# A wider second product of av, four warm-up products, combine weights kept once and the output in three column parts, under a new list of the first five engines

## The chip, the cores and the metric

The kernel runs on one core of one Trainium2 chip. The metric is the time of one execution on the device in microseconds (us), the median of several. TensorE is called PE below, its weight loads PEld, VectorE DVE, ScalarE ACT, GpSimd POOL, and SyncE, which issues all the DMAs of this kernel, SP.

## What is computed

Three stages follow one another on 3072 tokens of 512 columns, all in fp32.

```python
# attention: 4 batches x 8 heads x 768 tokens x 64; every query sees the keys within 16 of it
# and 24 block summaries (max of 32 keys, mean of 32 values)
a = softmax([mask(scale * q @ k.T), scale * q @ kmax.T + log(32)])
x = a @ [v, vmean]                          # then heads side by side: 3072 x 512
# dense layer, 512 -> 2048 -> 512
h = x @ w_in;  x = (h * cos(h)) @ w_out
# soft mixture of 8 experts with 4 slots each
logits = x @ phi                            # 3072 x 32
slots = softmax(logits, over tokens).T @ x  # 32 x 512
for e in range(8): out_e = relu(slots_e @ w1[e]) @ w2[e]      # 512 -> 1024 -> 512
y = softmax(logits, over slots) @ out       # 3072 x 512
```

## The kernel before

**Blocks and slots.** The tokens are cut into 6 blocks of 512, the 2048 hidden columns into 16 parts, which gives 96 slots s. A slot makes `h{s}a` and `h{s}c` (the product with `w_in`, lines 580, 581 and 588), `p`, `q` and `r` on DVE (lines 600, 604, 618), the sine `n{s}` and the cast `gh{s}` on ACT (608, 622), `gl{s}` on POOL (631) and `m{s}a`, `m{s}b` (the product with `w_out`). Each fp32 factor is split into a high part that ACT casts (`ih`, `oh`, line 553) and a low part (`il`, `ol`, line 560). Two PSUM banks hold the h products, so that `h{s+2}a` waits for `r{s}`.

**The sixteen weight parts** arrive as 1 MB loads `W{f}` and are unpacked during the first block by `ca`, `cb` on ACT (lines 134, 139), `cc` on DVE (148) and `cd` on POOL (156).

**Attention** runs in 24 groups. The first four (g = 0 to 3) have scores `sc{g}_{j}` (lines 327, 330), masking and maximum on DVE (`ev`, `mx`, lines 336, 344), exponentials in pieces of two query blocks on ACT (`ex`, line 366), a sum and reciprocal on DVE (`nm`), a normalisation on POOL (`nt`, line 456), transposes on PE (`tr`, 469) and their eviction (`aT`, 479). Then `av` multiplies by the 96 rows of values and `aw` by the 24 rows of block means, both at line 520: eight matmuls each per (g, j), with 64 columns. `xh` (ACT, line 536) and `xl` (DVE, 540) evict the result; `h0a` needs `xh` and `xl` of groups 0 and 2, `h0b` those of 1 and 3.

**The list.** Up to slot 80 the order of work of PE, DVE, ACT, POOL and SP is written out by hand: `ORDER` is a string of piece names, in which every engine executes its own pieces in the order in which they stand. The warm-up `fill_` (line 902) issues products of a matrix of ones; its four pieces f1, f11, f21 and f31 of ten matmuls stand ahead of `sc0_0` (two of them), behind `sc0_1` and behind `tr0_0`.

**The expert weights.** 64 blocks of 512 KB (`ex`) are loaded by `grab` into whatever space is free: 12 tiles that follow the attention's space when it closes, the spaces of xh and xl, those of the sixteen weight parts as the last block leaves them, 7 tiles of the ring, and x2 and x2T. The first 32 blocks are w1, the others w2. When a product has used a block, `release` either keeps its space for a later `place` or loads another block into it.

**The tail.** After the last slot come the logits and the softmax over tokens (the chain up to `slT`), `cT_mm` (transposes of the combine weights `call`, which stand there four times 32 columns wide: high, low, high, low), `hp_mm` (product with w1, line 1173), `relu`, `turn_h`, then the product with w2 in two halves of 256 columns (`yp_mm`, line 1219), `so_mm` (1239) and `combine` (line 1254, evicted at 1255, stored at 1256 as 512 KB with runs of 1024 bytes). Blocks 32 to 47 serve the first half and 48 to 63 the second.

Of the kernel before, what the change touches and what calls it, by code (L numbers as in the profile page):

```python
# [10 lines left out]
F32 = mybir.dt.float32  # L11
# [12 lines left out]
QB = 64  # L24
# [11 lines left out]
NFILL = 40  # L36
F0 = 10
# [8 lines left out]
NEXP = 12  # L46
# [27 lines left out]
def body(ctx: ExitStack, tc: tile.TileContext, q0, qk, kT, vT, vn, vx, w, phi, ex, cst, out):  # L74
# [430 lines left out]

    def first_av(g, j):
        first_x(g, j, grp[g]["v"][:KL, j], slice(0, KL))

    def first_aw(g, j):
        p = 2 * (g % 2) + j  # L510
        first_x(g, j, vsums[0][KL:KC, p:p + 1, :].to_broadcast([NSUM, 4, 128]), slice(KL, KC))

    def first_x(g, j, v, k):
        d = grp[g]
        if "av" not in d:
            d["av"], d["parts"] = bank(f"av{g}"), 0
        for u in range(4):
            for hh in range(2):
                r = slice(64 * hh, 64 * hh + 64)
                nc.tensor.matmul(d["av"][r, 256 * j + QB * u:256 * j + QB * u + QB], v[:, u, r],  # L520
                                 d["aT", j][k, 128 * u + 64 * hh:128 * u + 64 * hh + QB],
                                 start=d["parts"] == 0 and u == 0, stop=d["parts"] == 3 and u == 3)
        d["parts"] += 1

    def att_x(g):
        b, o = g // 4, 256 * ((g // 2) % 2)
        if b not in xh:
            xh[b] = xres.tile([128, 4, TB], F32R, name=f"xh{b}", tag="xh", bufs=2)
# [162 lines left out]
    call = m2.tile([128, 4 * NB, 4, 32], F32R, name="call", tag="call")  # L691
    run = {}

    def x2_out(j, t):
        do(f"xo{j}_{t}", x2_out_, t)

    def x2_out_(t):
        if x2 is None:
            m2_alloc_()
        if t % 2:  # L700
            return nc.scalar.mul(x2[:, t, :], acc[t], TWO_PI / W_SCALE)
        else:
            nc.vector.tensor_scalar_mul(x2[:, t, :], acc[t], TWO_PI / W_SCALE)
# [649 lines left out]
```

## Time and profile before

| | |
|---|---|
| median of 3 runs | 727.8 us (727.47 to 728.17) |
| the profiled execution | 730.21 us |
| its span, first to last instruction | 728.4 us |
| PE busy | 711.3 us (98%), 5260 matmul records |
| PEld busy | 560.0 us (77%) |
| DVE, ACT, POOL busy | 435.8 us, 411.5 us, 406.9 us |
| moved | 101.65 MB, of which HBM read 92.54 MB and written 6.29 MB |

The profiled execution took 1.8 us more than its span and 2.4 us more than the median of the runs. A busy share is an average over stages with different limits. An fp32 matmul leaves two records on PE, an fp32r matmul and a transpose one; matmuls are pipelined, so that the time per record is read from a run of them and not from the duration of one.

### The profile page before, as it was taken

The page shows a single profiled execution, that of the slowest core. Times are in us where ns is not written, and L with a number is a line of the kernel's source. Part 1 is how long each engine was busy: PE and PEld are TensorE (multiplying, and loading weights), DVE is VectorE, ACT ScalarE, POOL GpSimd, SP SyncE. Part 2 cuts the span into 40 slices and gives each one's busy share as a digit, 9 for nine tenths or more (in the row PEclk, how much of TensorE's full clock was granted, in tenths as well). Part 3 has the DMA queues.
Part 4 walks back from the last instruction along what each step waited for, and adds up shares of the span by engine and source line. Part 5 has one row for each costly group of instructions (what it writes and reads, how often), then busy time and mean ns, then how long its engine had stood idle before and what let it go on. Part 6 is the DMA issues. An engine that isn't in the chain of part 4 may idle for free.

```text
span 728.4 us, 13277 instructions
## 1 busy us (share of the span) xinstructions
PE 711.3 (98%) x5260; PEld 560.0 (77%) x5260; DVE 435.8 (60%) x680; ACT 411.5 (56%) x772; POOL 406.9 (56%) x310
## 2 busy tenths in 40 slices
PE   9899999999999999999999999999999999999994
PEld 9878777788887887787888787888787887787453
DVE  5678986974676574776574754674953444334323
ACT  4789997565554654654654754564735445434113
POOL 0756857766465565565673666674577665762000
PEclk9899999999999999999999999999999999999998
DMA  9976856402212301401302201301302822227998
GB/s 345 398 281 249 301 212 230 166 22 76 92 67 77 112 1 54 140 24 43 111 1 74 80 0 35 116 1 43 117 1 87 318 87 87 94 95 269 410 370 295
DMA packets 34862, 101.65 MB, mean 140 GB/s; under 512 B 3440, under 2 KB 13936, under 8 KB 32752
## 3 DMA queue, kind: packets, MB, share of 16 engines
q1 hardware_dynamic: 34800, 100.81, 38.1%
q8 instruction: 41, 0.67, 0.4%
q14 instruction: 21, 0.17, 0.1%
HBM read 92.54 MB, written 6.29 MB: 136 GB/s over the span
## 4 chain that ended last, share of the span: by engine, by line
PE 92%; ACT 4%; DVE 2%; issue 1%; POOL 0%
PE h L580 12%; PE h L581 12%; PE h L588 12%; PE acc L666 10%; PE acc L675 10%; PE acc L667 10%; PE tr L469 3%; PE av L504 3%; PE sc L384 2%; PE acc L652 2%; PE acc L653 2%; PE acc L655 2%; PE yp L1219 2%; PE hp L1173 2%; PE warmth L902 2%; PE av L520 1%
## 5 line engine op out<-in xcount | busy, mean ns | idle before, releaser
L631 POOL TENSOR_TENSOR gl<-a,gh 128x512 fp32r<-128x512 f32 x96 | 129.1, 1345 | 120.4 <-ACT gh L622 62.8
L560 POOL TENSOR_TENSOR wol<-w,woh 128x512 fp32r<-128x512 f32 x96 | 126.4, 1318 | 65.4 <-ACT woh L553 64.1
L580 PE MATMUL h<-xh,wih 128*128 128x512 f32 x384 | 155.4, 405 | 2.8 <-DVE a L618 2.8
L581 PE MATMUL h<-xl,wih 128*128 128x512 f32 x384 | 152.7, 398 | 0.0
L600 DVE TENSOR_SCALAR a<-h 128x512 f32<-128x512 f32 x96 | 66.0, 688 | 128.8 <-PE h L588 76.9
L608 ACT ACTIVATE a<-a,halfpi 128x512 f32<-128x512 f32 x96 | 69.4, 724 | 110.1 <-DVE a L604 109.8
L666 PE MATMUL acc<-woh,gh 128*128 128x512 f32 x320 | 127.4, 398 | 0.0
L667 PE MATMUL acc<-wol,gh 128*128 128x512 f32 x320 | 125.4, 392 | 0.0
L560 POOL TENSOR_TENSOR wil<-w,wih 128x512 fp32r<-128x512 f32 x81 | 106.9, 1323 | 30.0 <-PE h L588 11.4
L588 PE MATMUL h<-xh,wil 128*128 128x512 f32 x384 | 106.8, 401 | 0.0
L618 DVE TENSOR_TENSOR a<-h,a 128x512 f32<-128x512 f32 x96 | 65.9, 688 | 50.1 <-ACT a L608 50.1
L580 PEld LDWEIGHTS h<-xh,wih 128*128 128x128 f32 x384 | 72.3, 188 | 23.1 <-issue 3.7
L675 PE MATMUL acc<-woh,gl 128*128 128x512 f32 x320 | 88.3, 397 | 0.0
L581 PEld LDWEIGHTS h<-xl,wih 128*128 128x128 f32 x384 | 72.5, 189 | 16.0 <-DVE xl L540 0.5
L588 PEld LDWEIGHTS h<-xh,wil 128*128 128x128 f32 x384 | 71.0, 189 | 16.7 <-issue 1.0
L553 ACT CAST woh<-w 128x512 fp32r<-128x512 f32 x96 | 59.4, 619 | 32.1 <-PE acc L675 25.1
L553 ACT CAST wih<-w 128x512 fp32r<-128x512 f32 x96 | 59.3, 618 | 25.2 <-PE h L581 23.1
L622 ACT CAST gh<-a 128x512 fp32r<-128x512 f32 x96 | 58.9, 617 | 24.5 <-PE acc L667 19.1
L666 PEld LDWEIGHTS acc<-woh,gh 128*128 128x128 f32 x320 | 60.1, 188 | 14.4 <-issue 1.3
L667 PEld LDWEIGHTS acc<-wol,gh 128*128 128x128 f32 x320 | 60.2, 188 | 12.9
L675 PEld LDWEIGHTS acc<-woh,gl 128*128 128x128 f32 x320 | 58.8, 188 | 13.1 <-issue 0.6
L604 DVE SCALAR_TENSOR_TENSOR a<-a,h 128x512 f32<-128x512 f32 x96 | 65.5, 682 | 2.2
(156 smaller groups left out, 962.3 us busy)
## 6 DMA issues: line engine op xcount, KB each, us to landing
ex<-in_ex_dram SPq DMA_DIRECT2D x64, 512.0 KB
raw<-in_w_dram SPq DMA_DIRECT2D x16, 1024.0 KB
qk<-in_qk_dram SPq DMA_DIRECT2D x20, 736.0 KB
v<-in_vx_dram SPq DMA_DIRECT2D x24, 512.0 KB
kr<-in_kT_dram SPq DMA_DIRECT2D x16, 384.0 KB
out_dram<-o SPq DMA_DIRECT2D x12, 512.0 KB
vr<-in_vT_dram SPq DMA_DIRECT2D x12, 384.0 KB
v<-vs SPq DMA_DIRECT2D x40, 48.0 KB
```

The lines of the kernel that those rows point to most:

```text
L553: nc.scalar.copy(hi, W[f][:, part, :])
L560: (eng or nc.gpsimd).tensor_tensor(out=lo, in0=W[f][:, part, :], in1=hi, op=ALU.subtract)
L580: nc.tensor.matmul(h, hi[:, c], xh[s // NF][:, t, :], start=t == 0, stop=False)
L581: nc.tensor.matmul(h, hi[:, c], xl[s // NF][:, t, :], start=False, stop=False)
L588: nc.tensor.matmul(h, lo[:, c], xh[s // NF][:, t, :], start=False, stop=t == 3)
L600: nc.vector.tensor_scalar(out=a, in0=h, scalar1=0.25, scalar2=MAGIC, op0=ALU.add, op1=ALU.add)
L608: turn_dve["sin"] = nc.scalar.activation(a, a, AF.Sin, bias=halfpi, scale=-TWO_PI)
L618: nc.vector.tensor_tensor(out=a, in0=h, in1=a, op=ALU.mult)
L631: nc.gpsimd.tensor_tensor(out=gl, in0=a, in1=gh, op=ALU.subtract)
L666: nc.tensor.matmul(acc[t], gh[:, c], hi, start=f == 0, stop=False)
L667: nc.tensor.matmul(acc[t], gh[:, c], lo, start=False, stop=False)
L675: nc.tensor.matmul(acc[t], gl[:, c], hi, start=False, stop=f == NF - 1)
```

## The change

In the code, without the list:

```diff
-NFILL = 40
-F0 = 10
...
-NEXP = 12
+NEXP = 14
 NRING = 7
+PARTS = ((0, 256, 32), (256, 128, 48), (384, 128, 56))
...
     def first_av(g, j):
-        first_x(g, j, grp[g]["v"][:KL, j], slice(0, KL))
...
+                nc.tensor.matmul(d["av"][r, 256 * j + QB * u:256 * j + QB * u + QB], d["v"][:KL, j, u, r],
+                                 d["aT", j][:KL, 128 * u + 64 * hh:128 * u + 64 * hh + QB],
+                                 start=d["parts"] == 1 and u == 0, stop=False)
+
+    def first_aw(g, j):
+        d = grp[g]
         d["parts"] += 1
+        for hh in range(2):
+            r = slice(64 * hh, 64 * hh + 64)
+            a = d["aT", j][KL:KC, :].rearrange("p (u h c) -> p u h c", u=4, h=2)[:, :, hh, :]
+            nc.tensor.matmul(d["av"][r, 256 * j:256 * j + 256].rearrange("p (u c) -> p u c", u=4),
+                             vsums[0][KL:KC, 2 * (g % 2) + j, r], a, start=False, stop=d["parts"] == 4)
...
-    call = m2.tile([128, 4 * NB, 4, 32], F32R, name="call", tag="call")
+    call = m2.tile([128, 4 * NB, 2, 32], F32R, name="call", tag="call")
...
     def fill(n):
-        for i in range(0, n, 10):
-            do(f"f{i + (n > F0)}", fill_, min(10, n - i))
+        for i, k in enumerate((3,1,)):
+            do(f"f{i}", fill_, k)
 
     def fill_(n):
-        for i in range(n):
-            nc.tensor.matmul(warmth[:, 0:128], ones, ones, start=True, stop=True)
+        for _ in range(n):
+            nc.tensor.matmul(warmth, ones, ones.unsqueeze(1).to_broadcast([128, 4, 128]), start=True, stop=True)
...
         for i in range(NEXP):
             grab(exp_pool, f"e{i}")
+        grab(m2, "cT1")
...
-    for i in range(NRING):
+    for i in range(NRING + 1):
         grab(tail, f"r{i}")
...
     def cT_out(j):
-        o = cT[j // 2][:, 512 * (j % 2):512 * (j % 2) + 512]
-        (nc.scalar.copy if j % 2 else nc.vector.tensor_copy)(o, cps.pop(j))
+        o, ps = cT[j // 2][:, 512 * (j % 2):512 * (j % 2) + 512], cps.pop(j)
+        nc.vector.tensor_copy(o[0:64], ps[0:64])
+        nc.scalar.copy(o[64:128], ps[0:64])
...
-    cT_out(0)
-    cT_out(1)
     chain.__exit__(None, None, None)
...
-            release(16 * g + 4 * k + j, 2)
+            release(16 * g + 4 * k + j, 2 if g or k else 3)
...
     hp_mm(0, 0)
-    cT.append(place("cT2", F32R))
-    for j in range(2, 5):
+    cT += [place(f"cT{i}", F32R) for i in range(3)]
+    for j in range(5):
         cT_out(j)
...
-            u = 32 + 16 * h + 8 * g + 4 * (k // 4)
+            u = u0 + 4 * (8 // nk) * g + 4 * (k // nk)
...
-                                 eu[u + j][0][:, 256 * (k % 4):256 * (k % 4) + 256], start=k == 0, stop=k == 7)
-            if k % 4 == 3:
+                                 eu[u + j][0][:, w * (k % nk):w * (k % nk) + w], start=k == 0, stop=k == 7)
+            if k % nk == nk - 1:
...
     y_out(0, 1)
-    yp_mm(1, 0, range(2))
+    yp_mm(1, 0, range(4))
     so_mm(0, 0)
     so_mm(0, 1)
-    yp_mm(1, 0, range(2, 6))
+    yp_mm(1, 0, range(4, 8))
+    y_out(1, 0)
+    yp_mm(1, 1, range(3))
     for i in range(3):
         combine(0, i)
...
+    yp_mm(1, 1, range(3, 8))
     y_out(1, 1)
+    combine(0, 3)
     so_mm(1, 0)
     so_mm(1, 1)
-    for i in range(6):
-        combine(1, i)
+    combine(0, 4)
+    combine(0, 5)
+    yp_mm(2, 0, range(4))
+    combine(1, 0)
+    yp_mm(2, 0, range(4, 8))
+    y_out(2, 0)
+    yp_mm(2, 1, range(8))
+    y_out(2, 1)
+    combine(1, 1)
+    so_mm(2, 0)
+    so_mm(2, 1)
+    combine(1, 2)
+    for i in range(3):
+        combine(2, i)
```

So the second product `aw` issues two matmuls of 256 columns per (g, j) where it issued eight of 64. The warm-up is four matmuls of 512 columns, all ahead of `sc0_0`, where it was forty of 128 in four places. The combine weights stand once as high and low (64 columns), `cT_out` copies each turned block twice, and all three cT tiles take the places of blocks that the first `hp_mm` has used; this leaves room for two more `e` tiles, one more tile of the ring and one expert block at cT1's place. The output columns go as 256, 128 and 128: a `combine` of the last two parts makes eight products of 128 columns and stores 512 KB in runs of 512 bytes.

The new list holds the same pieces but for the warm-ups. The heads of three engines' lists, before (-) and after (+):

```diff
-PE  f1 f11 sc0_0 sc2_0 sc0_1 f21 sc2_1 sc1_0 sc1_1 sc3_1 sc3_0 tr0_0 f31 tr2_1 tr0_1 tr2_0 vs0_0 ...
+PE  f0 f1 sc0_0 sc0_1 sc2_0 sc2_1 sc1_0 sc1_1 tr0_0 sc3_0 sc3_1 vs0_0 tr0_1 vs0_1 vs0_2 av0_0 tr2_0 ...
-ACT ... ex3_0_0 aT0_1 cb1 xh2 xh0 ih0 aT1_1 ca2 aT3_1 cb2 ih1 xh3 xh1 ca3 cb3 ca4 cb4 ih2 y4_1 y4_0 n0
+ACT ... ex3_0_1 aT0_1 ca1 ih0 oh0 xh0 cb1 aT3_1 aT1_1 xh2 ca2 cb2 ih1 xh3 y4_1 xh1 y4_0 ca3 cb3 ih2 ca4 cb4 n0
-SP  K0 Q0 Q2 K1 C0 Q1 K3 C720 C848 K2 W0 K4 Q3 b0_0 W1 b0_2 b0_1 V2 V0 K5 V1 W2 V3 W3 W4 K6 G4 N G5 W5
+SP  K0 Q0 K1 C0 C848 Q2 K2 Q1 C720 K3 W0 V0 Q3 b0_0 b0_1 b0_2 V1 V2 W1 V3 K4 W2 G4 W3 W4 K5 G5 N W5
```

Up to `n8` ACT's list holds the same 112 pieces as before, in another order; up to `h10a` PE's list holds the same 85 pieces beside the warm-ups. On DVE, around `n8`, the list was `nm7 u9 q9 r8` and is `q9 r8 nm7 il10 nt7 r9 u9`.

## Rows read from the trace of the kernel before

**Rows 1.** Busy time by stage: stretch, engines (x instructions), granted PE clock, DMA share, GB/s.
```profile
0.00:41.20 41.20, 38.21 (x673) 36.47 (x674) 23.94 (x46) 24.94 (x81) 16.02 (x18) 0.92 0.92 353
41.20:104.00 62.80, 60.94 (x433) 47.42 (x433) 55.77 (x82) 62.34 (x138) 43.94 (x26) 1.00 0.74 268
104.00:110.00 6.00, 4.92 (x26) 3.72 (x28) 4.85 (x8) 4.88 (x7) 2.72 (x3) 0.72 0.51 194
...
250.00:400.00 150.00, 150.00 (x984) 119.68 (x983) 93.87 (x142) 83.50 (x140) 86.62 (x68) 1.00 0.17 57
680.00:700.00 20.00, 19.65 (x232) 9.02 (x232) 3.88 (x6) 2.85 (x5) 0.15 (x1) 1.00 1.03 411
706.00:708.00 2.00, 2.00 (x31) 1.37 (x33) 1.66 (x4) 1.40 (x3) 0.00 (x0) 1.00 0.45 161
720.00:722.00 2.00, 0.00 (x0) 0.00 (x0) 0.00 (x0) 0.00 (x0) 0.00 (x0) 1.00 1.03 340
```
**Rows 2.** Chain of waits, 0 to 42 us: start, us, what.
```profile
1.08 7.31 PE warmth L902 x40
...
11.89 2.43 PE warmth L902 x20
...
20.65 2.23 PE warmth L902 x20
...
28.25 1.90 issue
30.16 3.24 PE av L520 x48
33.40 3.60 PE tr L469 x16
...
41.20 0.59 ACT xh L536
```
**Rows 3.** Waits of ACT, 0 to 42 us: who waited for whom, total us, times, longest.
```profile
ACT S L366 <- DVE mx L344: 9.3, 2, 8.8
ACT xh L536 <- PE av L520: 6.1, 4, 2.3
```
**Rows 4.** PE in order of time, 24 to 28.3 us: start, duration, line, operands, records.
```profile
24.23 1.52 PE L215 MATMUL vs<-vb,avg 128*32 128x128 f32 x48
25.68 1.62 PE L520 MATMUL av<-aT,v 96*64 96x64 f32 x48
27.23 1.03 PE L520 MATMUL av<-aT,vs 24*64 24x64 f32 x28
```
**Rows 5.** Single microseconds of the first stage, columns as in group 1.
```profile
5.00:6.00 1.00, 1.00 (x7) 1.00 (x6) 0.00 (x0) 0.00 (x0) 0.00 (x0) 1.00 0.98 322
21.00:22.00 1.00, 1.00 (x11) 1.00 (x11) 1.00 (x2) 1.00 (x7) 1.00 (x1) 1.00 1.04 424
31.00:32.00 1.00, 1.00 (x19) 0.88 (x18) 0.04 (x1) 0.59 (x1) 1.00 (x1) 0.50 1.06 385
```
**Rows 6.** DMA queues, 27 to 29 us: queue, kind, packets, MB, share of 16 engines.
```profile
q8 instruction: 1, 0.02, 3.0%
```
**Rows 7.** All engines in order of time around the end of ACT's full stretch.
```profile
101.64 0.72 ACT L608 ACTIVATE a<-a,halfpi 128x512 f32<-128x512 f32 x1
...
102.83 0.90 DVE L199 TENSOR_REDUCE ks<-kr 128x24 f32<-128x768 f32 x1
...
104.25 0.68 DVE L618 TENSOR_TENSOR a<-h,a 128x512 f32<-128x512 f32 x1
...
105.08 0.47 PE L580 MATMUL h<-xh,wih 128*128 128x512 f32 x1 [1.81 <-DVE a L618]
```
**Rows 8.** PE in order of time in the tail, the product with w2 and the combine.
```profile
692.68 3.64 PE L1219 MATMUL yp<-ex,hT 128*32 128x256 f32 x64
...
705.07 1.70 PE L1254 MATMUL op<-so,cT 128*128 128x256 f32 x12
```
**Rows 9.** SP's last part, in order of time, and its last wait.
```profile
706.45 16.51 SPq L1256 DMA_DIRECT2D out_dram<-o  x12
...
SPq L1349 <- DMA out_dram<-o: 4.4, 1, 4.4
```

More of the change, by code (lines that the diff above doesn't have):

```diff
@@ L516, in first_x @@
             d["av"], d["parts"] = bank(f"av{g}"), 0
+        d["parts"] += 1
         for u in range(4):
@@ L812, in m2_wn @@
         nc.vector.tensor_tensor(out=c, in0=c, in1=run["cs", j].unsqueeze(2).to_broadcast([128, 4, 32]), op=ALU.mult)
-    def m2_cs(j):
-        return (run["c", j].unsqueeze(2).to_broadcast([128, 4, 2, 32]),
-                call[:, 4 * j:4 * j + 4].rearrange("p t (a b) s -> p t a b s", b=2))
     def m2_wh(j):
-        c2, o = m2_cs(j)
-        nc.scalar.copy(o[:, :, :, 0], c2)
+        nc.scalar.copy(call[:, 4 * j:4 * j + 4, 0], run["c", j])
     def m2_wl(j):
-        c2, o = m2_cs(j)
-        nc.gpsimd.tensor_tensor(out=o[:, :, :, 1], in0=c2, in1=o[:, :, :, 0], op=ALU.subtract)
+        o = call[:, 4 * j:4 * j + 4]
+        nc.gpsimd.tensor_tensor(out=o[:, :, 1], in0=run["c", j], in1=o[:, :, 0], op=ALU.subtract)
     def m2_c(j):
@@ L1072, in cT_mm @@
         for t in range(4):
-            nc.tensor.transpose(ps[:, 128 * t:128 * t + 128],
-                                call[:, 4 * j + t].rearrange("p r s -> p (r s)").bitcast(F32), ident)
+            nc.tensor.transpose(ps[0:64, 128 * t:128 * t + 128],
+                                call[:, 4 * j + t].rearrange("p b s -> p (b s)").bitcast(F32), ident)
     def cT_out(j):
-        o = cT[j // 2][:, 512 * (j % 2):512 * (j % 2) + 512]
-        (nc.scalar.copy if j % 2 else nc.vector.tensor_copy)(o, cps.pop(j))
+        o, ps = cT[j // 2][:, 512 * (j % 2):512 * (j % 2) + 512], cps.pop(j)
+        nc.vector.tensor_copy(o[0:64], ps[0:64])
+        nc.scalar.copy(o[64:128], ps[0:64])
     cps = {}
-    cT = [tail.tile([128, 1024], F32R, name="cT0", tag="cT0"), m2.tile([128, 1024], F32R, name="cT1", tag="cT1")]
+    cT = []
     chain = tc.manual_schedule(engines={EE.PE, EE.DVE, EE.Activation})
@@ L1225, in y_out @@
     def y_out(h, g):
-        nonlocal ys, so, places
+        nonlocal ys, so
         if ys is None:
@@ L1229, in y_out @@
             so = place("so", F32R)[:, 0:512]
-        c = slice(256 * h, 256 * h + 256)
-        (nc.scalar.copy if g else nc.vector.tensor_copy)(ys[g][:, c], yps[h, g])
+        c0, w, _ = PARTS[h]
+        (nc.scalar.copy if g else nc.vector.tensor_copy)(ys[g][:, c0:c0 + w], yps[h, g])
     so_ps = {}
     def so_mm(h, g):
-        c = slice(256 * h, 256 * h + 256)
+        c0, w, _ = PARTS[h]
+        c = slice(c0, c0 + w)
         if g == 0:
-            so_ps[h] = ps_h.tile([128, 512], F32, name=f"so_p{h}", tag="h")[:, 0:256]
+            so_ps[h] = ps_h.tile([128, 512], F32, name=f"so_p{h}", tag="h")[:, 0:w]
         nc.tensor.matmul(so_ps[h], sel[:, 32 + 128 * g:160 + 128 * g], ys[g][:, c], start=g == 0, stop=g == 1)
@@ L1245, in combine @@
         nonlocal turn_o
-        c = slice(256 * h, 256 * h + 256)
-        o = place(f"o{h}_{i}").rearrange("p (t c) -> p t c", c=256)
+        c0, w, _ = PARTS[h]
+        c = slice(c0, c0 + w)
+        o = place(f"o{h}_{i}")
+        n_t, n_p = 1024 // w, 512 // w
         for t in range(2):
@@ L1251, in combine @@
             ps = pool.tile([128, 512], F32, name=f"op{h}_{i}_{t}", tag=tag)
-            for n in range(2):
-                k = 512 * (i % 2) + 256 * t + 128 * n
-                nc.tensor.matmul(ps[:, 256 * n:256 * n + 256], cT[i // 2][:, k:k + 128], so[:, c], start=True, stop=True)
-            (nc.scalar.copy if t else nc.vector.tensor_copy)(o[:, 2 * t:2 * t + 2, :].rearrange("p t c -> p (t c)"), ps)
-        nc.sync.dma_start(out=out[512 * i:512 * i + 512, c].rearrange("(t p) c -> p t c", p=128), in_=o)
+            for n in range(n_p):
+                k = n_t * i + n_p * t + n
+                nc.tensor.matmul(ps[:, w * n:w * n + w], cT[k // 8][:, 128 * (k % 8):128 * (k % 8) + 128], so[:, c], start=True, stop=True)
+            (nc.scalar.copy if t else nc.vector.tensor_copy)(o[:, 512 * t:512 * t + 512], ps)
+        nc.sync.dma_start(out=out[128 * n_t * i:128 * n_t * (i + 1), c].rearrange("(t p) c -> p t c", p=128),
+                          in_=o.rearrange("p (t c) -> p t c", c=w))
     yp_mm(0, 0, range(8))
@@ L1262, in body @@
     y_out(0, 1)
-    yp_mm(1, 0, range(2))
+    yp_mm(1, 0, range(4))
     so_mm(0, 0)
     so_mm(0, 1)
-    yp_mm(1, 0, range(2, 6))
+    yp_mm(1, 0, range(4, 8))
+    y_out(1, 0)
+    yp_mm(1, 1, range(3))
     for i in range(3):
         combine(0, i)
-    yp_mm(1, 0, range(6, 8))
-    y_out(1, 0)
-    yp_mm(1, 1, range(6))
-    for i in range(3, 6):
-        combine(0, i)
-    yp_mm(1, 1, range(6, 8))
+    yp_mm(1, 1, range(3, 8))
     y_out(1, 1)
+    combine(0, 3)
     so_mm(1, 0)
     so_mm(1, 1)
-    for i in range(6):
-        combine(1, i)
+    combine(0, 4)
[12 more added lines that the diff above has]
+        combine(2, i)
     order.__exit__(None, None, None)
@@ L1329, in _layout @@
     e1 = moe2_w1.reshape(2, 4, 4, 128, FF).transpose(0, 2, 1, 3, 4).reshape(32, 128, 1024)
-    e2 = moe2_w2.reshape(2, 4, 2, 4, 128, 2, 256).transpose(5, 0, 2, 1, 4, 3, 6).reshape(32, 128, 1024)
+    e2 = []
+    for c, n, _ in PARTS:
+        x = moe2_w2[..., c:c + n].reshape(2, 4, n // 128, 1024 // n, 128, n)
+        e2.append(x.transpose(0, 2, 1, 4, 3, 5).reshape(-1, 128, 1024))
     return dict(
```

19 lines of the change are left out of this document (7 added, 12 removed).

## The prediction

> **What bounds the kernel now.** I read the table of busy time by stage first, then the chain of waits in the stage where engines stand idle, then who waits for whom there, and last the DMA share of the tail.
>
> From 110 to 668 us PE does its work without a gap; in the stretch shown it is busy 150.00 of 150.00 us at the full granted clock [rows 1]. That work stays: the list moves matmuls there, it removes none. What is to be won lies ahead of it or behind it.
>
> Between 41.2 and 104 us two engines are full at once: PE 60.94 of 62.80 us, ACT 62.34 of 62.80 us [rows 1]. ACT never pauses there, and at its end PE waits for it: the sine of slot 8 starts at 101.64, DVE's multiply at 104.25, and the next product h at 105.08, after 1.81 us of idle PE [rows 7]. So in this stretch ACT is the pace, and the stretch begins when ACT gets its last late input, xh at 41.20 [rows 2].
>
> Before 41.2 us ACT is busy only 24.94 us [rows 1], idle 16.26. Its waits say why: 8.8 us for the first maximum (9.3 in two waits), 6.1 us for av's results from PE [rows 3]. And the chain says what PE did meanwhile: warm-up products for 7.31, 2.43 and 2.23 us, a stop of 1.90 us, then av and tr at a slow pace [rows 2].
>
> In the tail PE is again nearly always at work (19.65 of 20.00 us at 680 to 700), while the DMA engines are full, at 411 GB/s for 4096-byte runs and 340 GB/s for the 1024-byte runs of the output [rows 1]. The twelve output DMAs are issued from 706.45 on, and SP's last wait, 4.4 us, is for the last of them [rows 9]. The end is set by the time of the first output and the price of twelve.
>
> **The warm-up.** Forty records of 128 columns are replaced by eight of 512 ahead of the scores: 5120 columns become 4096, a saving of 1024 columns, eight old records. PE handles some 7 records in a microsecond at first and 11 later [rows 5]; a record at the later pace costs 2.43 / 20 = 0.12 us [rows 2]. What is dropped comes off the fast end, 8 x 0.12 = 1.0 us. The first scores, the first maximum and ACT's first exponential move by that 1.0 us, since the mask is loaded earlier in the new list and DVE has nothing else by then. The pieces f21 and f31 go too: 2.43 + 2.23 = 4.66 us off PE's chain [rows 2].
>
> **The second product.** A record of av or aw with 64 columns costs 1.62 / 48 = 0.034 and 1.03 / 28 = 0.037 us [rows 4]; the two heads of a pair work side by side. All of aw is 64 matmuls, 128 records, 4.7 us. The new form has 32 records of 256 columns. If columns bind, a pair costs what a record of 256 columns would, twice the 0.12 of a 128-column one, 16 x 0.24 = 3.9 us; if the two heads no longer overlap it is 7.7 us. I take 3.9, because the nearest row, av, shows that such pairs overlap: -0.8 us, with +3.0 as the other end.
>
> **PE's chain in the head.** 41.2 - 1.0 - 4.7 - 0.8 = 34.7 us if everything else repeats itself. But two losses hang on circumstance. At 28.25 PE stands still for 1.90 us with no wait in the profile [rows 2], and a 16 KB instruction fetch is among the DMA packets just then [rows 6]; PE has 673 + 674 records of matmuls and weight loads by 41.2 us [rows 1] and will have 336 fewer (144 of the warm-up, 192 of aw). And the granted clock is 0.50 (1.2 of 2.4 GHz) at 31 us, after that stop [rows 5]; a mean of 0.92 over 41.2 us [rows 1] is 6.6 us at the lower level, of which half is lost, 3.3 us: tr then takes 3.60 us for 16 records [rows 2]. Without both the chain ends at 29.5 us.
>
> **What ACT makes of it.** ACT's list holds the same pieces up to n8, so that only its idle time can change. Gone at most: 1.0 of the first wait, the 0.5 of the second maximum, and the 6.1 for av, together 7.6 us; xh of group 3 would follow at 33.6 us, later than PE's 29.5, earlier than 34.7. So PE will bind in part. The loads keep up: 350 to 360 GB/s [rows 1] bring W3, 12.1 MB into the new list, at 34 to 35 us, where ACT comes to it. I take 6.3 of the 7.6 us, and 3.5 to 7.6 as the bounds: the lower one where PE stops and slows as it did. This gain is kept to 104 us because ACT is full all the way.
>
> **At the hand-over to PE.** Between n8 and h10a DVE did nm7 and u9 (0.90 us, [rows 7]) ahead of r8; now r8 comes first. PE waited 1.81 us and then ran at half clock, 0.72 on the mean of 104 to 110 us [rows 1], another 1.7 us. All of that, 3.5 us, would go if PE came no earlier; but PE comes earlier by more than ACT does, so that it waits for ACT anyway. I take 0.7, from 0 to 3.5.
>
> **Everything in between.** Slots 10 to 80 hold the same matmuls in another order; PE has no slack there, so I take 0 and leave -0.5 to +1.5 for a wait that the list adds or removes. Smaller copies of the combine weights (six pieces on ACT and POOL) lie beside PE's work: 0.
>
> **The tail.** Three more blocks loaded during the last slots take 3 x 1.28 us off the stream of loads (512 KB at 411 GB/s, [rows 1]); worth 0, as hp and yp run at PE's pace with their blocks there before them. `cT_out` moves behind the first hp product: five copies on DVE and five on ACT beside the three hp products that stand ahead of relu, 0; without that cover relu would be 1 to 2 us later. The narrow yp: 128 records of 0.057 us [rows 8] become 256 of 128 columns. A product of that very shape is vs, 1.52 / 48 = 0.032 us [rows 4], so 7.3 becomes 8.1 us; at the old price per record it would be 14.6. Ahead of the first combine stand 88 such records (2.8 us) where 48 wide ones stood (2.7 us): the first output leaves at 706.5 as before. Narrow op products: 48 at 0.07 to 0.14 us (1.70 / 12 = 0.14, [rows 8]); eight of them, 1.1 us, are shorter than the transfer of their output. So from 708 us on, the outputs queue. An output of 1024-byte runs takes 512 KB / 340 GB/s = 1.54 us, and of 512-byte runs more: a packet costs one of 16 engines 48 ns at 1024 bytes and 160 ns at 4096 [rows 1], a line that gives 29 ns at 512 bytes, 1.9 us for an output. 6 x 1.54 + 6 x 1.9 = 20.6 us from 708.2, end at 728.8 where it was 727.5. The DMA's gaps of before (0.45 of full at 706 to 708, [rows 1]) are counted in the old end and not in the new: +1.0 us, from -1.5 to +2.5.
>
> The Trainium skill (DMA: Bandwidth & Descriptors, Specifications) puts the shortest transfer at line rate at 512 bytes and sees trouble only below. By that rule a 512-byte output would take 1.28 us and the tail would end about 2.7 us before its old end. The trace disagrees already at 1024 bytes, 340 against 411 GB/s [rows 1]; no row shows 512-byte stores.
>
> **The sum.** -6.3 - 0.7 + 0 + 1.0 = -6.0 us. The profiled execution (730.2) would take 724.2; the median of the runs lies 2.4 below it, 721.8.
>
> **The rivals.** (A) The head's gain is given back: with fewer products PE is less busy at 18 to 33 us, the clock falls to 0.50 there, or the fetch stops PE again. For it: both happened before, in the same stretch [rows 2, 5, 6]. Against: fewer instructions, no warm-up pieces between. ACT then gains 3.5, less 0.5 in later waits, and the tail costs 1.0: -2.0 to -3.5, about 725.0. The skill (Runtime: NRT & Kernel Launch, Instruction fetch mechanics) calls such a fetch mostly hidden, by which the stop of 1.90 us would not be one; the row of the fetch speaks against the rule here [rows 6].
>
> (B) No change: DMA supply, at a share of 0.92 until 41.2 us [rows 1], gates av or the unpacking as late as before, and ACT's waits only change their name. Against: V0, V1 and V3 stand 1.8 to 3.8 MB earlier in the new list. Within 1.4 us of 727.8.
>
> (C) A short run costs no more per byte than a 1024-byte one, or the first output leaves earlier: the tail gives 1 to 1.5 us instead of costing 1, and PE avoids the slow clock at 105 us: -9, 718.8.
>
> (D) Slower: in slots 10 to 80 a list that puts a sine late behind an exponential costs PE what it cost at 102.9 us, 1.81 idle and 1.7 at half clock, 3.5 us a time. There are eight pairs of groups with such an exponential; from two late ones on (7 us) the gain is gone; with three: -6.0 + 10.5 = +4.5, 732.3. For it: h waits for the sine two slots back. Against: before, the same stretch shows no such stop [rows 1].
>
> **How the numbers follow.** Forecast (719.5 to 724) 0.50; A 0.20; B 0.10; C 0.10; D and its kin 0.10. A measurement of this kernel tells 0.2%, 1.5 us, from no change. Faster 0.80 (forecast, A and C), same 0.10 (B), slower 0.10 (D). Range: 718.5 to 726.3, which leaves out most of B, all of D and the far end of C.
>
> **What would show it.** Right: ACT's idle time before 41 us falls from 16 to about 10 us, xh of group 3 comes at 34 to 36 us, ACT stays full to some 98 us, h10a starts at 97 to 99; first output issued as early before the end as now or 1 us earlier; outputs of 512-byte runs 1.9 us apart. Wrong: a stop of PE or a clock of 0.50 between 20 and 35 us that ACT waits for; PE idle after 110 us; outputs 1.3 or over 2.5 us apart. The prediction fails if ACT is not the pace until 104 us after all, for then the gain of the head isn't handed on.

## The result and the profile after

The changed kernel takes 721.2 us, the median of four runs (720.9 to 722.06); the kernel before took 728.0 beside it (727.47 to 732.91). The ratio is 0.9893 (95% interval 0.985 to 0.9937). The profiled execution took 722.06 us with a span of 720.3; before it was 730.21 and 728.4. So the profiles show 8.1 us and the medians 6.8. The median of the kernel before lies between 726.9 and 729.2 in the four sessions of this study, that of the changed kernel at 721.2 and 720.8 in two; a difference of about 1 us between medians of different sessions says little.

First the table by stage of the kernel after: stretch, length, then busy time and instructions of PE, PEld, DVE, ACT and POOL, the granted PE clock, the DMA share and GB/s. It answers [rows 1]; the stages are the same, a few us earlier.

```profile
0.00:34.00 34.00, 29.72 (x496) 22.81 (x498) 23.32 (x44) 24.08 (x80) 14.68 (x17) 0.95 0.96 374
41.20:94.00 52.80, 51.07 (x371) 40.09 (x361) 48.74 (x71) 51.81 (x122) 37.52 (x23) 1.00 0.83 304
98.00:104.00 6.00, 6.00 (x56) 4.75 (x55) 5.68 (x8) 4.98 (x9) 4.15 (x3) 1.00 0.39 128
250.00:400.00 150.00, 150.00 (x1054) 119.95 (x1056) 94.98 (x141) 82.27 (x146) 89.09 (x67) 1.00 0.15 50
680.00:700.00 20.00, 19.65 (x327) 12.75 (x320) 5.11 (x9) 4.32 (x10) 0.00 (x0) 1.00 0.75 294
711.00:718.00 7.00, 0.00 (x0) 0.00 (x0) 0.00 (x0) 0.34 (x1) 0.00 (x0) 0.55 0.99 286
```

ACT does in 34 us nearly all of what took it 41 us before (24.08 us of work against 24.94 [rows 1]). In the stretch behind the hand-over PE is busy 6.00 of 6.00 us at the full granted clock, where it was 4.92 at 0.72 [rows 1]. The last row is new: outputs with 512-byte runs at 286 GB/s, where 1024-byte runs went at 340 [rows 1].

The waits of ACT in the first 45 us, which answer [rows 3]: who waited for whom, total us, times, longest.

```profile
ACT S L365 <- DVE mx L343: 7.7, 3, 7.2
ACT w L133 <- DMA raw<-in_w_dram: 1.4, 1, 1.4
```

The 6.1 us for av are gone. A wait of 1.4 us for the first weight part is new.

PE in order of time at the end of the head: start, duration, line, operands, records. This answers the av and tr pieces of [rows 2] and the pace of [rows 4].

```profile
27.71 1.08 PE L523 MATMUL av<-aT,vs 24*64 24x256 f32 x8
28.73 1.96 PE L468 MATMUL tr<-ident,S 128*120 128x128 f32 x16
30.62 0.65 PE L523 MATMUL av<-aT,vs 24*64 24x256 f32 x4
31.19 2.08 PE L513 MATMUL av<-aT,v 96*64 96x64 f32 x64
33.21 1.94 PE L523 MATMUL av<-aT,vs 24*64 24x256 f32 x16
35.08 0.50 PE L581 MATMUL h<-xh,wih 128*128 128x512 f32 x1
```

Sixteen transposes take 1.96 us where they took 3.60 at half clock [rows 2], sixteen wide records of aw 1.94, and h0a starts at 35.08 where it started at 41.08.

The engines around the hand-over, which answer [rows 7]: the sine of slot 8, DVE's multiply, PE's last m and h10a.

```profile
95.82 0.73 ACT L609 ACTIVATE a<-a,halfpi 128x512 f32<-128x512 f32 x1
96.58 0.69 DVE L619 TENSOR_TENSOR a<-h,a 128x512 f32<-128x512 f32 x1 [0.80 <-ACT a L609]
...
96.88 1.18 PE L676 MATMUL acc<-woh,gl 128*128 128x512 f32 x4
97.89 0.40 PE L581 MATMUL h<-xh,wih 128*128 128x512 f32 x1
```

DVE's multiply follows the sine at once, 0.76 us from start to start where it was 2.61, and PE comes to h10a without a gap. In the tail, PE's narrow products, the issues of the outputs by SP and SP's last wait answer [rows 8, 9]:

```profile
702.78 2.83 PE L1216 MATMUL yp<-ex,hT 128*32 128x128 f32 x96
705.53 1.11 PE L1254 MATMUL op<-so,cT 128*128 128x128 f32 x8
```

```profile
697.24 17.25 SPq L1256 DMA_DIRECT2D out_dram<-o  x12
```

```profile
SPq L1363 <- DMA out_dram<-o: 4.7, 1, 4.7
```

The issues begin at 697.24 where they began at 706.45, and the last wait is 0.3 us longer.

The next table splits each trace at four starts: h0a, h10a, h12a and the first `hp` product; us each. All kernels of this study are in it; they are told of below.

| kernel | median | start of h0a | h0a to h10a | h10a to h12a | h12a to hp | hp to end |
|---|---|---|---|---|---|---|
| before | 728.0 | 41.08 | 63.99 | 11.99 | 559.54 | 51.84 |
| after | 721.2 | 35.08 | 62.81 | 10.01 | 559.65 | 52.74 |
| after_again | 720.8 | 33.56 | 62.20 | 10.01 | 560.56 | 52.71 |
| narrow_aw | 723.3 | 37.93 | 64.04 | 10.01 | 559.70 | 52.64 |
| old_warmup | 724.0 | 37.72 | 61.89 | 10.01 | 559.69 | 52.68 |
| old_list | 724.4 | 35.54 | 64.85 | 10.43 | 559.59 | 52.74 |
| two_parts | 719.4 | 33.24 | 62.15 | 10.02 | 559.67 | 52.02 |
| two_again | 719.2 | 32.83 | 62.29 | 10.02 | 559.66 | 52.00 |
| two_few | 719.5 | 33.51 | 62.00 | 10.02 | 559.67 | 51.78 |
| after_swap | 722.5 | 34.89 | 63.31 | 10.11 | 559.69 | 52.75 |
| before_swap | 726.1 | 39.37 | 63.08 | 10.82 | 559.61 | 51.81 |
| act_more | 722.0 | 33.50 | 63.91 | 10.10 | 559.67 | 52.75 |
| act_four | 725.3 | 35.09 | 65.88 | 10.11 | 559.66 | 52.76 |
| pool_four | 722.9 | 34.90 | 64.70 | 10.02 | 559.99 | 52.74 |

After less before: -6.00 in the head, -1.18 and -1.98 around the hand-over, +0.11 in the middle, +0.90 in the tail, together -8.15 us, the difference of the spans.

### The profile page after: what moved, and what is told of

It is laid out like the page before. It is cut to its first block, busy times and chain, and to the rows that moved or that the text cites. A ratio compares the mean times of both kernels' runs of the same rounds, so it can differ in the third digit from the quotient of the medians.

```text
span 720.3 us, 13293 instructions
## 1 busy us (share of the span) xinstructions
PE 703.6 (98%) x5248; PEld 552.0 (77%) x5248; DVE 442.9 (61%) x685; ACT 411.5 (57%) x777; POOL 411.1 (57%) x310
## 4 chain that ended last, share of the span: by engine, by line
PE 90%; ACT 4%; DMA 3%; DVE 1%; issue 0%; SPq 0%
PE h L581 12%; PE h L582 12%; PE h L589 12%; PE acc L667 10%; PE acc L676 10%; PE acc L668 10%; PE av L503 3%; PE tr L468 3%; PE sc L383 2%; DMA raw<-in_w_dram 2%; PE acc L653 2%; PE acc L654 2%; PE yp L1216 2%; PE acc L656 2%; PE hp L1168 2%; PE xt L713 1%
## 5 line engine op out<-in xcount | busy, mean ns | idle before, releaser
L632 POOL TENSOR_TENSOR gl<-a,gh 128x512 fp32r<-128x512 f32 x96 | 131.0, 1366 | 114.6 <-ACT gh L623 69.0
L561 POOL TENSOR_TENSOR wol<-w,woh 128x512 fp32r<-128x512 f32 x96 | 127.9, 1335 | 81.7 <-ACT woh L554 75.2
L561 POOL TENSOR_TENSOR wil<-w,wih 128x512 fp32r<-128x512 f32 x81 | 108.5, 1345 | 17.3 <-ACT wih L554 8.9
L589 PE MATMUL h<-xh,wil 128*128 128x512 f32 x384 | 105.1, 398 | 0.0
L554 ACT CAST wih<-w 128x512 fp32r<-128x512 f32 x96 | 59.2, 619 | 28.3 <-PE h L582 18.4
```

The source lines that it names most:

```text
L554: nc.scalar.copy(hi, W[f][:, part, :])
L561: (eng or nc.gpsimd).tensor_tensor(out=lo, in0=W[f][:, part, :], in1=hi, op=ALU.subtract)
L589: nc.tensor.matmul(h, lo[:, c], xh[s // NF][:, t, :], start=False, stop=t == 3)
L632: nc.gpsimd.tensor_tensor(out=gl, in0=a, in1=gh, op=ALU.subtract)
```

## The experiments

The first four undo one part of the change each and share a chip and the runs of the kernel before (median 728.29 there). The changed kernel itself was not run beside them: "over the changed kernel" compares with its 721.2 from the session of the result. By the ratios to the kernel before, 0.9893 for the changed kernel, the losses of the next three come out larger, some 3.4, 4.1 and 3.6 us, so that their sizes are good to about 1 us.

**narrow_aw** puts the eight products of 64 columns back.

```diff
-        for hh in range(2):
-            r = slice(64 * hh, 64 * hh + 64)
...
+        first_x(g, j, vsums[0][KL:KC, p:p + 1, :].to_broadcast([NSUM, 4, 128]), slice(KL, KC))
```

> The changed kernel, with the second product of av again as eight matmuls of 64 columns. Theory: PE's chain in the head gets 0.8 us longer (4.7 us of records against 3.8), and since xh follows the last of these products at once, ACT gets its last input up to 0.8 us later and the kernel takes 0.3 to 0.8 us more, 721.5 to 722.0. Rival: 192 more instructions starve PE of its instructions again, a stop of some 1.9 us and the lower clock: 724 to 726.

Measured: 723.31 us (722.14 to 726.11, nine runs), ratio to before 0.994 (0.9923 to 0.9958), 2.1 us over the changed kernel: above what the theory allows for the products alone, just short of the rival. The trace is that of its slowest execution, and it shows both losses that the rival names. PE stood still ahead of h0a, and the granted clock was 0.50 twice:

```profile
33.70 2.08 PE L519 MATMUL av<-aT,vs 24*64 24x64 f32 x64
37.93 0.58 PE L579 MATMUL h<-xh,wih 128*128 128x512 f32 x1 [2.16 <-ACT w L133]
```

```profile
28.00:31.00 3.00, 3.00 (x15) 2.73 (x13) 2.58 (x5) 2.06 (x4) 2.65 (x2) 0.50 1.01 420
38.00:41.00 3.00, 3.00 (x8) 2.32 (x8) 0.94 (x2) 0.66 (x1) 2.26 (x1) 0.50 0.63 195
```

```profile
q8 instruction: 1, 0.02, 2.1%
```

The first fence is PE in order of time, the second the table by stage, the third the DMA queues of 35 to 38 us. The profile names ACT's unpacking as what ended the stop; but in the changed kernel, with the same list, h0a starts at 35.08 and that piece of ACT at 35.92, so h0a doesn't need it. A 16 KB instruction fetch lies in the stop, as it did in the stop of the kernel before [rows 2, 6]. That the fetch is the cause is argued, not shown. The products themselves cost less than the theory has it: the 64 records of 64 columns in the first fence take 2.08 us where sixteen wide ones did the same work in 1.94, both at the full granted clock. Over all of aw the wide form saves about 0.3 us so, and not 0.8. What else is lost in the median is the stop and the slow clock, or something that this one trace doesn't show.

**old_warmup** puts forty products of 128 columns back in four places, f21 and f31 behind `sc0_1` and `tr0_0`.

```diff
-        for i, k in enumerate((3,1,)):
-            do(f"f{i}", fill_, k)
+        for i in range(0, n, 10):
+            do(f"f{i + (n > 10)}", fill_, min(10, n - i))
```

> The changed kernel, with the forty narrow warm-up products of before in their four places (two ahead of the first scores, one behind the second scores, one behind the first transposes). Theory: the first exponential comes 1.0 to 1.6 us later and the other two pieces, 4.7 us of PE, lengthen the chain to xh; ACT idles for most of it: 3 to 6 us more, 724 to 727. Rival: PE has slack in the new head, only the first 1.0 to 1.6 us count: 722.2 to 722.8.

Measured: 723.98 us (723.34 to 725.1, eight runs), ratio 0.995 (0.9933 to 0.9968), 2.8 us over the changed kernel. Just at the theory's lower end. ACT's waits in the head, in the columns of the view above:

```profile
ACT S L365 <- DVE mx L343: 11.7, 4, 8.1
```

Four us more than after, one wait of 8.1 for the first maximum and two of 1.66 and 1.75 us where PE made warm-up products while DVE waited for scores. h0a starts 2.64 us later than in the changed kernel's first trace and 4.16 later than in after_again; at the end, by the table, 1.77 and 2.95 us are left of it. Most of the loss of the head arrives at the end.

**old_list** keeps all the code of the change and takes the list of before (without f21 and f31).

```diff
-ORDER = """zz1 kz0 kz3 kz2 kz1 K0 f0 Q0 K1 C0 C848 Q2 K2 Q1 u0 C720 K3 f1 W0 u1 sc0_0 ...
+ORDER = """kz1 kz3 kz2 kz0 K0 f0 Q0 Q2 K1 C0 Q1 f1 K3 C720 u0 C848 K2 sc0_0 W0 sc2_0 ...
```

> The changed kernel with the list of before (its two wide warm-up pieces where the first two narrow ones stood). Theory: warm-up and second product alone take 1.0 + 4.7 + 0.8 us off PE's chain ahead of xh, and the lost stop and clock may go with them, so ACT's last input comes 4 to 7 us earlier than before; the hand-over at slot 10 stays as it was (multiply of slot 8 behind two other pieces on DVE), so that 2 to 3 us of the gain are missing: 723 to 725.5. Rival: the gain comes from the order of the loads and of ACT's pieces; then the old list keeps most of the old time, 726 to 728.

Measured: 724.36 us (720.75 to 726.68, ten runs), ratio 0.9943 (0.9922 to 0.9963), 3.2 us over the changed kernel, as the theory has it. Its executions lie far apart, though, and the fastest is as fast as the changed kernel. In its trace the head costs 0.5 us; the rest is lost between h0a and h12a, 75.28 us where after takes 72.82. PE waits ahead of h10a for 2.62 us and is busy 3.61 of 6.00:

```profile
100.39 0.47 PE L581 MATMUL h<-xh,wih 128*128 128x512 f32 x1 [2.62 <-DVE a L619]
...
98.00:104.00 6.00, 3.61 (x34) 2.83 (x36) 5.51 (x9) 5.71 (x10) 2.58 (x2) 1.00 0.54 191
```

**two_parts** stores the output in two parts of 256 columns, in the old order of the tail.

```diff
-PARTS = ((0, 256, 32), (256, 128, 48), (384, 128, 56))
+PARTS = ((0, 256, 32), (256, 256, 48))
```

> The changed kernel, with its output again in two parts of 256 columns in the old sequence of the tail. Theory: the outputs queue at the end, and six of 512-byte runs cost 1.75 us each in the changed kernel's trace where 1024-byte ones cost 1.54; with two parts the kernel is 0.5 to 1.3 us faster than the changed one (721.2), about 720.3. Rival: three parts shorten what follows the last weights, and the capacity for three more blocks pays only with them; then two parts are 1 to 2 us slower, 722.2 to 723.2.

Measured: 719.36 us (718.7 to 720.46, six runs), ratio 0.9884 (0.9863 to 0.9905). Better than both kernels, and on the theory's side, by more than it forecast. The stretch from the first hp to the end is 0.72 us shorter than after's (52.02 to 52.74). The last six outputs go at 341 GB/s, the rate of 1024-byte runs [rows 1], where the changed kernel stores at 286:

```profile
709.00:715.00 6.00, 0.00 (x0) 0.00 (x0) 0.00 (x0) 0.00 (x0) 0.00 (x0) 0.73 1.04 341
```

The medians differ by 1.8 us, more than that.

Then the hand-over and the pace, beside runs of before with a median of 726.92.

**after_swap** puts `nm7` and `u9` back ahead of `q9` and `r8` on DVE.

```diff
- ... cc11 p9 q9 r8 nm7 il10 nt7 r9 u9 ...
+ ... cc11 p9 nm7 u9 q9 r8 il10 nt7 r9 ...
```

> The changed kernel, but with the two steps nm7 and u9 put back ahead of q9, r8 and il10 in VectorE's order, as the old list has them; nothing else moves. Theory: at 96 us VectorE is what PE waits for, and the new order there gave about 2 us. nm7 waits for the last exponential of group 7 (it took 2.32 us so, and 0.20 for the reciprocal), and u9 takes 0.9 us, so that r8 comes 1.0 to 2.0 us later, PE gets a gap ahead of h10a, and all that follows moves with it: 722.2 to 723.2 us, and up to 724.9 if the granted clock falls after the gap, against 721.2 for the changed kernel. Rival: the gap at h10a went because PE and ScalarE arrive there otherwise, not through VectorE's order: 720.7 to 721.7.

Measured: 722.52 us (721.13 to 728.59, seven runs), 1.35 us over the changed kernel. That is the theory's range, but three of the seven executions (721.13 to 721.52) lie in the rival's, and the ratio's interval is wide (0.9952, 0.9918 to 0.9987). So the times don't decide. The trace shows the mechanism, DVE first, then PE:

```profile
93.83 1.98 DVE L448 TENSOR_SCALAR sm<-sm 128x8 f32<-128x8 f32 x1
95.84 0.20 DVE L450 RECIPROCAL rs<-sm 128x8 f32<-128x8 f32 x1
95.96 0.90 DVE L198 TENSOR_REDUCE ks<-kr 128x24 f32<-128x768 f32 x1
96.78 0.68 DVE L605 SCALAR_TENSOR_TENSOR a<-a,h 128x512 f32<-128x512 f32 x1
97.38 0.68 DVE L619 TENSOR_TENSOR a<-h,a 128x512 f32<-128x512 f32 x1
```

```profile
98.21 0.47 PE L581 MATMUL h<-xh,wih 128*128 128x512 f32 x1 [1.29 <-DVE a L619]
```

The sum of the exponentials stands on DVE for 1.98 us, the reduction of the next keys for 0.90, and the multiply that PE waits for comes behind both. PE has a gap of 1.29 us where after has none. The clock stayed at 1.00 behind it.

The sum isn't long because it waits for the exponential, as the expectation has it: in the kernel before its last exponential releases it at 100.36 us, after 0.17 us of waiting, and it takes 2.32 us from there. What goes on beside it is POOL's piece of the unpacking, `cd`. These are the two instructions in the kernel before, in after_swap and in after:

```profile
100.28 2.37 POOL L156 TENSOR_TENSOR w<-w,cv 128x1024 int32<-128x1024 int32 x1 [2.14 <-DVE w L148]
100.36 2.32 DVE L449 TENSOR_SCALAR sm<-sm 128x8 f32<-128x8 f32 x1 [0.17 <-ACT S L438]
...
93.38 2.40 POOL L155 TENSOR_TENSOR w<-w,cv 128x1024 int32<-128x1024 int32 x1 [1.70 <-DVE w L147]
...
94.54 2.39 POOL L155 TENSOR_TENSOR w<-w,cv 128x1024 int32<-128x1024 int32 x1 [1.69 <-DVE w L147]
97.19 0.16 DVE L448 TENSOR_SCALAR sm<-sm 128x8 f32<-128x8 f32 x1
```

Where the sum starts while POOL's instruction runs, it ends 0.03 us behind that instruction's end (102.68 and 102.65, 95.81 and 95.78); in after it starts when POOL is done and takes 0.16. So it is in the whole trace of the kernel before: ten of the sum's 23 records take more than 0.2 us, and each of the ten starts inside an instruction of POOL and ends within 0.05 us behind its end. What the new order does is to put `r8` ahead of an instruction that POOL holds up.

**before_swap** does the reverse in the kernel before.

```diff
- ... cc11 nm7 u9 q9 r8 il10 ...
+ ... cc11 q9 r8 nm7 u9 il10 ...
```

> The kernel before, with q9 and r8 moved ahead of nm7 and u9 in VectorE's order; nothing else moves. Theory: r8 starts 1.0 to 2.0 us earlier than at 104.25, the gap of 1.81 us ahead of h10a closes, and the stretch at half clock behind it goes or shrinks (1.7 us of loss): 724.5 to 726.8 us against 728.0. Rival: the sine of slot 8, which ends at 102.3, or another product is what h10a waits for: 727.5 to 728.5.

Measured: 726.09 us (725.1 to 729.23, ten runs) against 726.92, ratio 0.9997 (0.9976 to 1.0019): no change that can be measured. The interval leaves room for a gain of 1.7 us, the lower part of what the theory forecast, and for none, as the rival has it. The trace of this one execution shows a gain: the gap ahead of h10a is 0.88 us where it was 1.81 [rows 7], the clock behind it is 1.00 where it was 0.72 [rows 1], and the stretch from h0a to h12a is 73.90 us instead of 75.98.

```profile
100.86 0.72 ACT L608 ACTIVATE a<-a,halfpi 128x512 f32<-128x512 f32 x1
101.61 0.69 DVE L618 TENSOR_TENSOR a<-h,a 128x512 f32<-128x512 f32 x1 [1.87 <-ACT a L608]
...
102.45 0.48 PE L580 MATMUL h<-xh,wih 128*128 128x512 f32 x1 [0.88 <-DVE sm L449]
```

```profile
104.00:110.00 6.00, 5.90 (x55) 4.44 (x54) 5.95 (x9) 6.00 (x10) 3.60 (x3) 1.00 0.67 227
```

Of the 2.1 us, 0.9 is the gap and 1.2 lies behind it. The gap that is left is the sine's, as in the rival: the multiply now follows it at once, and PE is there before. Trace and times can both be right if the fall of the clock at 105 us doesn't come in every execution of the kernel before. Only one of these has a trace, so this stays open.

**act_more** and **act_four** issue the activation of line 133 twice, for two weight blocks and (with `(6, 7, 8, 9)`) for four.

```diff
-        nc.scalar.activation(W[f], raw[f][:, :, :, 1].bitcast(F32), AF.Prelu, scale=2.0 ** -111, alpha=-2.0 ** 32)
+        for _ in range(2 if f in (8, 9) else 1):
+            nc.scalar.activation(W[f], raw[f][:, :, :, 1].bitcast(F32), AF.Prelu, scale=2.0 ** -111, alpha=-2.0 ** 32)
```

> The changed kernel with the activation of line 133 issued twice for the weight blocks 8 and 9 (the second writes the same values): two more instructions of 1.15 us on ScalarE between slots 6 and 8. Theory: ScalarE sets the pace until the sine of slot 8, so that h10a comes 1.5 to 2.3 us later and the end with it: 722.7 to 723.5 us against 721.2. Rival: PE or the loads set the pace by then and ScalarE's time is covered: 720.7 to 721.7.

> The changed kernel with the activation of line 133 issued twice for the weight blocks 6 to 9: four more instructions of 1.15 us, 4.6 us of ScalarE between slots 5 and 8. With two of them the span from h0a to h10a grew by 1.85 us in the trace, and the median by 0.8 to 722.0. Theory (ScalarE is the pace until the sine of slot 8): the span from h0a to h10a grows by 3.8 to 4.6 us over 62.0 to 62.8, and the median is 724.0 to 725.8. Rival (part of it is covered, PE or the loads being nearly as late): 722.3 to 723.5.

Measured: 721.97 us (721.47 to 722.51, six runs) and, on another chip beside after_again, 725.26 (723.75 to 731.3, twelve runs), 0.8 us over the changed kernel's 721.2 and 4.4 over after_again. The first falls between theory and rival, the second is the theory's. The traces are plainer than the medians: over the 62.20 us of after_again the span from h0a to h10a grows by 1.71 us for 2.3 us of work on ACT and by 3.68 for 4.6. The trace of act_four has a stretch at half clock in the head, as after's has, and over the 62.81 us of after the growth is 3.07. So two thirds to four fifths of what ACT gets to do arrive at PE.

**pool_four** issues POOL's subtraction `gl` twice for slots 2 to 5.

```diff
-        nc.gpsimd.tensor_tensor(out=gl, in0=a, in1=gh, op=ALU.subtract)
+        for _ in range(2 if s in (2, 3, 4, 5) else 1):
+            nc.gpsimd.tensor_tensor(out=gl, in0=a, in1=gh, op=ALU.subtract)
```

> The changed kernel with GpSimd's subtraction gl issued twice for slots 2 to 5: four more instructions of 1.36 us, 5.4 us of GpSimd in the same stretch. Theory (ScalarE is the pace there, GpSimd is busy 37.5 of 52.8 us and has room): no change beyond 0.7 us, 720.5 to 721.9. Rival (any engine's time counts there, since each is nearly full): 723 to 726.

Measured: 722.87 us (722.51 to 729.01, nine runs), 2.0 us over after_again. The theory misses: POOL's time counts there too. The span from h0a to h10a grows by 2.50 us for 5.4 us of work (by 1.89 over after, which has a stretch at half clock in the head as pool_four has), so that a third to a half arrives. The rows: the stage for pool_four and for after_again, and pool_four's waits of ACT and of DVE at 41 to 100 us.

```profile
41.20:94.00 52.80, 49.58 (x353) 38.82 (x354) 47.62 (x67) 49.91 (x113) 43.64 (x27) 1.00 0.80 291
```

```profile
41.20:94.00 52.80, 51.75 (x367) 41.17 (x367) 49.10 (x71) 52.56 (x125) 38.27 (x24) 1.00 0.85 308
```

```profile
ACT a L609 <- DVE a L605: 2.2, 2, 1.6
ACT xh L537 <- PE av L503: 0.6, 1, 0.6
...
DVE a L601 <- POOL gl L633: 2.7, 2, 1.6
```

The path can be read there. DVE's first step of a slot (`p`) writes a buffer that an earlier `gl` has to read first, and waits 2.7 us for POOL; ACT's sine waits 2.2 us for DVE in turn, and ACT idles 2.8 us in all, where it waited for nothing in after_again. The run makes `gl` come later as well as POOL fuller, and doesn't tell the two apart. A mean of 38 busy us in 53 says little of what waits for each instruction.

**two_few** is two_parts with 11 `e` tiles for early blocks instead of 14: three of the four places that the change added are gone.

```diff
-NEXP = 14
+NEXP = 11
```

> The version with the output in two parts of 256 columns, with 11 blocks of the last products loaded early instead of 14, as before the change. Theory (the three more blocks are worth nothing, since the products run at PE's pace with their blocks there ahead of them): 718.9 to 719.9 us, as with 14 (719.4). Rival: the early blocks keep loads away from the output's start, each 1.28 us of transfer: 720.5 to 723.

Measured: 719.51 us (718.76 to 722.39, four runs), hp to end 51.78 where two_parts has 52.02: the three blocks are worth nothing, as forecast. With the output in three parts this wasn't run.

**after_again** and **two_again** run the changed kernel and two_parts side by side (before: 729.22).

> The changed kernel once more, on the same chip as the three beside it, for comparison and for how far its own executions lie apart. Expected: a median of 721.2 us, 720.5 to 722. If a stretch of TensorE at 1.2 GHz in the head comes in some executions and not in others, the profile shows h0a either at 33.2 to 33.5 us (as in the traces of two_parts, act_more and two_few, without it) or near 35 us (as in the changed kernel's first trace, with it).

> The version with the output in two parts of 256 columns once more, on the same chip as the changed kernel, to size the cost of the three parts. Theory (outputs of 512-byte runs take 1.7 us each where 1024-byte runs take 1.5, and the last of them ends the kernel): 0.7 to 2.0 us below the changed kernel, 719.2 to 720.5. Rival (the 1.8 us seen between the medians came from the chip or the session): within 0.5 us of the changed kernel.

Measured: 720.83 us (719.69 to 726.34, six runs; ratio 0.9897, 0.9869 to 0.9926) and 719.21 (718.58 to 720.49, four runs; ratio 0.9869, 0.9846 to 0.9892). So two parts beat three by 1.6 us again. Of that the tail shows 0.71 in the traces (52.00 to 52.71). The two traces lie 2.24 us apart; what is more than the tail's lies in the head (0.73) and the middle (0.90), where both kernels have the same list and where the changed kernel's first trace has no such 0.90 (559.65). So that part differs between executions of one kernel. Why the medians differ by more than the tail's 0.7 is open.

## Why the prediction was right

The forecast was 721.8, and the time is 721.2. Its terms, one by one, for the profiled pair:

**Head: -6.3 forecast, -6.00 measured.** The reason holds too: ACT's idle time up to 41.2 us fell from 16.3 to 9.9 us (about 10 was forecast), xh of group 3 was done at 35.2, and ACT was then full but for one wait until n8. The 6.3 us are made up a little otherwise than in the sum: 1.6 from the waits for the maxima (1.5 forecast) and all 6.1 of av, less a new wait of 1.4 for a weight part, which the sum didn't have. Taken back one at a time, the warm-up costs 2.8 us, the wide aw 2.1 and the list 3.2, each as medians. The first two are seen in the start of h0a (2.6 and 2.9 us later than in after); the list's loss is mostly the hand-over's, with 0.5 in the head. These losses need not add up to the gain.

**The wide aw: 3.9 us for 32 records forecast; 1.94 us for sixteen, 3.9, measured.** The two heads overlap, and the upper end of +3.0 is out. The saving of 0.8 was too high all the same, because the old form was priced too dear: a record of 64 columns cost 2.08 / 64 = 0.033 us in narrow_aw and not 1.03 / 28 = 0.037, so that about 0.3 us was to be saved.

**Clock and fetch in the head.** These made the width of the head's term, and rightly. Rival A was half true: the changed kernel's first trace has the clock at 0.50 from 18.8 to 22.2 us, after_again has not.

```profile
19.00:22.00 3.00, 3.00 (x45) 2.53 (x44) 2.18 (x6) 3.00 (x18) 1.13 (x2) 0.50 1.05 431
```

```profile
19.00:22.00 3.00, 2.94 (x73) 2.18 (x68) 2.96 (x8) 3.00 (x17) 2.22 (x2) 1.00 1.04 423
```

(The rows are the table by stage, after first, then after_again.) Nine traces share the whole new head. Four of them have one such stretch, after and, at 27 to 30 us, after_swap, act_four and pool_four; h0a starts at 34.9 to 35.1 us in these and at 32.8 to 33.6 in the five others. So a head with a fall of the clock to 1.2 GHz ends 1.3 to 2.3 us later here. Not all of that need be the clock's: PE in after also stands idle for 1.7 us ahead of the fall, where after_again has 0.7. What brings the fall on in one execution and not in the next stays open, for after_swap has it with no idle over 0.7 ahead. The Trainium skill (Runtime: NRT & Kernel Launch, Instruction fetch mechanics) calls instruction fetch mostly hidden. In the changed kernel's trace that agrees, fetches land at 28 and 35 us and PE goes on; the stops of 1.90 us before [rows 2, 6] and of 2.16 us in narrow_aw, each with a fetch inside, would disagree if the fetch is their cause, which no run shows.

**Hand-over: -0.7 forecast, -3.16 measured (1.18 + 1.98).** This is the term that was mis-sized. Its mechanism was right, `r8` waited behind `nm7` and `u9`; the step that failed is "PE comes earlier by more than ACT does, so that it waits for ACT anyway". PE does not wait at h10a any more: the gap of 1.81 us is closed, and the fall of the clock behind it, 1.7 us, didn't come. PE came earlier by less than ACT: the last m ahead of h10a ended 5.2 us earlier (103.27 and 98.06), the sine started 5.8 earlier (101.64 and 95.82). Nor was the gap the sine's, as the first part of the prediction and rival D have it: the sine had ended 1.9 us before DVE's multiply began [rows 7]. after_swap and before_swap put DVE's order at 0.6 us (h0a to h12a against after; 1.2 against after_again) and at up to 2.1 us in their traces; in times the first shows 1.35 and the second nothing clear of noise. old_list, which takes back every move of the list, loses 2.46 us there. How the 3.16 divides between DVE's order, the other moves and the clock isn't shown. It was within the bound given, 3.5.

**ACT as the pace until 104 us: right, but not alone.** act_four hands on 3.1 to 3.7 of 4.6 us. pool_four shows that POOL's time counts too, and the sum behind POOL's instruction (after_swap) is a second way from POOL to PE, which the prediction did not see; it gave the smaller copies on POOL as free, and they are in the tail, where that was true.

**Middle: 0 forecast, +0.11 measured.** Rival D, late sines behind exponentials, did not come: PE was busy 150.00 of 150.00 us in the stretch shown.

**Tail: +1.0 forecast, +0.90 measured.** The parts: 512-byte outputs 1.9 us forecast, 1.8 by the rate of 286 GB/s; narrow yp 0.032 us a record forecast, 2.83 / 96 = 0.029 measured; eight op products 1.1 us forecast, 1.11 measured; the first output at 697.24, 9.2 us earlier than 706.45 [rows 9], where the first hp is 9.0 earlier; from that issue to the end 23.1 us, 1.1 more than before, while the 708.2 from which the sum lets the outputs queue stands in no row; the early blocks 0, as two_few shows for three of them with the output in two parts. The Trainium skill (DMA: Bandwidth & Descriptors, Specifications) has line rate from 512 bytes on; the trace disagrees, 286 GB/s at 512 bytes, where stores of 1024 bytes had 340 and loads of 4096 bytes 411 [rows 1]. By that rule a 512-byte output would take 1.28 us (an estimate, 512 KB at 411 GB/s), less than the 1.54 of a 1024-byte one, and three parts would have ended earlier than two; they ended 0.7 us later. Rival C, that a short run costs no more per byte, is out by the two rates.

**Profile and median.** The forecast for the profiled execution was 724.2, it took 722.06. The 2.1 us too much are the hand-over's (2.5), less 0.3 of the head. In the median they are not seen, because the profiled execution of before lay 2.4 us over its median and that of after 0.9: a part of what the hand-over gave in the profile was, it seems, never in the median of before. That the forecast of the median came within 0.6 us is luck in part: the sum gave 2.1 us too little, and carrying the 2.4 us between profile and median over to the changed kernel, where it was 0.9, gave 1.5 too much.

## What to carry to other kernels

Look for the engine that idles first and is full ever after: of a microsecond won in its idle time most arrives at the end (1.77 of 2.64 us and 2.95 of 4.16 in old_warmup). Put what the next engine waits for ahead of what merely has to be done, on every engine between them; a step that is held up there holds up all behind it, as DVE's sum of eight columns did for 2 us beside POOL's piece. And a split that makes the last stores shorter must be paid from the store rate at that size, read from a row and not from the line rate.

## What was not expected of the hardware

The granted clock fell for a stretch in the head in one trace of the changed kernel and not in the other (19 to 22 us, 0.50 and 1.00, above), with h0a at 35.08 and 33.56. POOL, busy 38.27 of 52.80 us, passed on 2.50 of 5.4 us of added work: a share of 72% covered only about half of it. And DVE's sum of 128x8, 0.16 us alone, took up to 2.32 us when it started during an instruction of POOL, and ended when that did.
